# All of v loaded from Pool's queue, and the output tile's pad columns cleared by DVE

## Chip, cores and metric

The kernel runs on 1 core of one Trainium2 chip. The metric is the device time of one execution in microseconds. Before the change the median of 3 runs is 1309.79 us (1308.56 to 1313.95).

## What is computed

Three stages follow each other, all in float32. The change lies in the first.

```python
def _attn_ref(q, k, v):                  # q, k, v: 8 batches, 8 heads, 576 tokens, 64 wide
    chunk = 64
    scores = (q_c @ k_c^T) / sqrt(64)    # within each chunk of 64 tokens
    attn = exp(scores - max) / (sum + 1e-9)
    return attn @ v_c

def _moe_ref(x, w_skip, w_gate, w1, w2): # x: 4608 tokens x 512
    do_compute = x @ w_skip > 0
    e_idx = argmax(x @ w_gate)           # one of 8 experts
    y = gate_w * (relu(x @ w1[e]) @ w2[e])
    return where(do_compute, x + y, x)

def _moe2_ref(x, w_in, w_out):           # 512 -> 2048 -> 512
    h = x @ w_in
    return where(h >= 1, h, where(h <= -1, 0, (h + 1) ** 2 / 4)) @ w_out
```

## The kernel before

**Attention and routing** work on units of 256 tokens, 18 of them (NU), four chunks each. One pass of the loop `for i in range(NU - 1)` handles several units in different steps of their way. s_T transposes q and k of unit i+2 on TensorE and e_T copies them out of PSUM, s_SC makes the scores of unit i+1 and e_SC their exponent on ACT, s_ET and e_ET transpose unit i's exponents, s_AV multiplies them with v of unit i and writes the normalised result into the output tile xn, s_XT transposes xn of unit i-1, s_LG makes the logits of unit i-2. s_SEL and s_RANK choose each token's expert and its place in that expert's list. Their short DVE instructions go into a queue `fill`, from which dve() puts one behind each longer DVE instruction.

**Loads.** load_qk brings q on SP's queue and k on ACT's, two units ahead of their transposes, into tiles with two buffers. load_v brings v on SP's queue: eight loads for a unit, one for each of the four chunks and each parity of the head (line 281), 64 partitions x 4 heads x 64 elements, 64 KB. They go into one of three tiles vbd, in which two heads stand beside each other on a block diagonal, with a column of ones for the sum. load_v(i + 2) stands near the head of pass i; its tile is free once s_AV of unit i-1 has read it.

**The output tile** xn (tag xn, 4 buffers) is 128 partitions x 2 x 516: 512 columns of the token, the gate in column 512 and padding. s_AV gets it and clears columns 512 to 515 with a memset on Pool (line 383); DVE then writes the 512 columns (line 401). Some units later f_gate writes the gate (line 501) and put_x sends the whole tile to x_dram in HBM by a DMA from Pool's queue (line 508). The unit that comes four later needs that buffer again. After the put, f_put scatters the unit's token numbers into the experts' lists, by two indirect DMAs from Pool's queue of 128 single elements each (line 579).

**What sets the order.** The program is written inside `tc.manual_schedule()`: instructions stand on each engine in the order of the code. Each engine works through its own list in order, and a DMA is issued by the engine that it is written on (SP, ACT or POOL), after what that issue waits for. At the start Pool clears a k tile, two of the vbd tiles and some small ones, and issues five small DMAs.

**After attention** come the experts one after another (weights as a sum of two parts, three matmuls for each product), and the last feed-forward stage. They need the routing to be complete.

Of the kernel before, what the change touches and what calls it, by code (L numbers as in the profile page):

```python
# [19 lines left out]
NT, DM = B * S, H * D  # L20
# [7 lines left out]
ROW = DM + 4  # L28
# [58 lines left out]
def kernel(ctx, tc, q, k, v, w_skip, w_gate, w1, w2, w_in, w_out, consts, out):  # L87
    nc = tc.nc
# [16 lines left out]
    def big():  # L105
        return ps.tile([P, 1024], F32, tag="big", name="big", bufs=3)
# [21 lines left out]
    def runs(t0, n):  # L128
        done = 0
        while done < n:  # L130
            b, s = divmod(t0 + done, S)
            step = min(n - done, S - s)
            yield done, step, b, s
            done += step

    def mm(o, l, r, start=True, stop=True):
        nc.tensor.matmul(out=o, lhsT=l, rhs=r, start=start, stop=stop)  # L137
# [120 lines left out]
    T = {}  # L258
# [14 lines left out]
    def load_v(u):  # L273
        if u >= NU:
            return
        for off, n, b, s in runs(u * UNIT, UNIT):
            c0, c1 = off // CH, (off + n) // CH
            for c in range(c0, c1):
                s0 = s + (c - c0) * CH
                for par in range(2):  # L280
                    nc.sync.dma_start(
                        out=vbds[u % NV][64 * par:64 * par + 64, c, :, par, 0:D],
                        in_=v[b, par:H:2, s0:s0 + CH, :].rearrange("h p d -> p h d"),
                    )
# [3 lines left out]
    def dve(n=1):  # L288

        for _ in range(n):  # L290
            if fill:
                fill.pop(0)()
# [83 lines left out]
    def s_AV(u, s):  # L376
        if not 0 <= u < NU:
            return
        et = T["et", u]
        vb = vbds[u % NV]  # L380
        if s == 0:
            T["x", u] = x_p.tile([P, 2, ROW], F32, tag="xn", name="xn", bufs=4)
            nc.gpsimd.memset(T["x", u][:, :, DM:ROW], 0.0)
        xn = T["x", u]
        b = big()
        bg = b.rearrange("p (g w) -> p g w", g=2)[:, :, 0:2 * VW]
        for hp in range(HP):
            for cc in range(2):
                o = (hp % 2) * VW
                mm(  # L390
                    bg[64 * cc:64 * cc + 64, hp // 2, o:o + VW],
                    et[:, s, hp, cc * CH:cc * CH + CH],
                    vb[:, 2 * s + cc, hp].rearrange("p a w -> p (a w)"),
                )
        b4 = bg.rearrange("p g (h w) -> p g h w", w=D + 1)
        rc = r_p.tile([P, 2, H // 2, 1], F32, tag="rc", name="rc")
        nc.vector.tensor_scalar(out=rc, in0=b4[:, :, :, D:D + 1], scalar1=1e-9, scalar2=None, op0=ALU.add)
        dve()
        nc.vector.reciprocal(out=rc, in_=rc)
        dve()  # L400
        nc.vector.tensor_tensor(
            out=xn[:, s, 0:DM].rearrange("p (g h d) -> p g h d", g=2, d=D),
            in0=b4[:, :, :, 0:D],
            in1=rc.to_broadcast([P, 2, H // 2, D]),
            op=ALU.mult,
        )
# [398 lines left out]
    with tc.manual_schedule():  # L805
# [28 lines left out]
        for u, nm, eng in ((0, "qu", nc.scalar), (0, "ku", nc.vector), (1, "qu", nc.scalar)):  # L834
            s_T(u, nm)
            for r in range(2):
                e_T(u, nm, r, eng)
        load_qk(2)
        load_v(0)
        s_T(1, "ku")  # L840
        for r in range(2):
# [4 lines left out]
        nc.gpsimd.tensor_copy(cb, c0[:, C_TRI:C_SEL])  # L846
        load_qk(3)
        load_v(1)
        late = []
        for i in range(NU - 1):  # L850
            s_T(i + 2, "qu")
            s_T(i + 2, "ku")
            load_qk(i + 4, ("qu",))
            load_v(i + 2)
            s_ET(i)
            e_T(i + 2, "qu", 0)
# [15 lines left out]
            if i + 2 == NU:  # L872
                step()
                late.append(fill.pop())
            s_AV(i, 0)
            s_AV(i, 1)
            if i + 2 == NU:
                put_x(i, T["x", i], slice(0, DM))
# [9 lines left out]
        u = NU - 1  # L888
# [10 lines left out]
        run(a[2:6], fill[:3] + r[:1])  # L899
        fill[:] = fill[3:] + a[6:]  # L900
        s_AV(u, 0)
        run(b[:2])
        s_AV(u, 1)
# [380 lines left out]
```

## Time and profile before

| | |
|---|---|
| median of 3 runs | 1309.79 us |
| profiled execution | 1305.73 us, span 1303.9 us |
| TensorE busy | 1238.8 us (95%) |
| DVE, ACT busy | 680.6 us (52%), 662.6 us (51%) |
| POOL busy | 228.9 us (18%), 277 instructions |
| v loads | SP's queue, 144 of 64 KB |
| DMA queues | q1 (SP) 117.30 MB, q10 (ACT) 56.19 MB, q0 (POOL) 28.20 MB |

The span is the time from the first to the last instruction of the profiled execution; the execution's own time is 1.83 us longer. Issuing a DMA is not counted as busy time, except that the rows list each issue with its start and length. In a row of waits the engine named first stood idle until the one behind the arrow was done; where that is a DMA, until the DMA had landed. Queue q1 is SP's, q10 ACT's, q0 Pool's; their rows give packets, MB and the time of these packets as a share of 16 DMA engines.

### The profile page before, as it was taken

To read this page: it belongs to the slowest core of one execution; us is meant where nothing else is said; L and a number is where in the kernel's file an instruction comes from. 1 tells how busy PE (TensorE), PEld (TensorE's weight loads), DVE (VectorE), ACT (ScalarE), POOL (GpSimd) and SP (SyncE) were. 2 spreads that over 40 slices of the span, in tenths; PEclk is the share of its full clock that TensorE was granted. 3 is DMA by queue.
4 is the path that set the end of the run, shared out by engine and by line. 5 is a ranking of instruction groups with operands and counts; after the bars stand their busy time and mean duration, and the time that the engine had idled before them with its cause. 6 is when DMAs were issued, how large, how long until landed. Compare 5 with 4: busy or idle time off the path is not lost.

```text
span 1303.9 us, 19838 instructions
## 1 busy us (share of the span) xinstructions
PE 1238.8 (95%) x7126; PEld 1042.4 (80%) x7128; DVE 680.6 (52%) x1308; ACT 662.6 (51%) x1115; POOL 228.9 (18%) x277
## 2 busy tenths in 40 slices
PE   7987868899999989999999999999999999999998
PEld 6876755789889978888888888887888888888887
DVE  5765686467776691221121120003776687668665
ACT  7875763354444312232223222225787678668764
POOL 3122246434434271011111111000000000000000
PEclk9988996899999999999999999999999999999999
DMA  9989974578776565443344333235343343334431
GB/s 237 232 175 178 189 160 156 124 233 279 218 251 220 170 201 177 161 170 135 132 160 152 119 134 127 108 120 149 111 129 121 114 121 124 119 116 119 127 115 41
DMA packets 163067, 202.98 MB, mean 156 GB/s; under 512 B 51274, under 2 KB 88421, under 8 KB 162966
## 3 DMA queue, kind: packets, MB, share of 16 engines
q1 hardware_dynamic: 107254, 117.30, 33.0%
q10 hardware_dynamic: 45136, 56.19, 12.8%
q0 software_dynamic: 10576, 28.20, 6.4%
q8 instruction: 57, 0.93, 0.3%
q14 instruction: 44, 0.36, 0.1%
HBM read 135.88 MB, written 66.48 MB: 155 GB/s over the span
## 4 chain that ended last, share of the span: by engine, by line
PE 74%; DVE 3%; DMA 2%; issue 1%; ACT 1%; SPq 0%; ACTq 0%; DVEq 0%
PE b L137 30%; PE a L137 30%; PE bank L137 6%; PE big L137 5%; PE t L140 1%; DMA stg<-in_moe_w_dram 1%; DVE a L192 1%; DVE a L191 1%; DMA stg<-in_moe_w_in_dram 1%; DVE s L193 0%; PE t L137 0%; PE big L688 0%; DVE bl L166 0%; DVE hl L717 0%; DMA xs<-x_dram 0%
## 5 line engine op out<-in xcount | busy, mean ns | idle before, releaser
L137 PE MATMUL b<-bh,xh 128*128 128x512 f32 x576 | 225.1, 391 | 1.7 <-ACT xh L1183 1.7
L137 PE MATMUL b<-bh,xl 128*128 128x512 f32 x576 | 225.1, 391 | 0.0
L137 PE MATMUL b<-bl,xh 128*128 128x512 f32 x576 | 224.2, 389 | 0.0
L137 PE MATMUL a<-xh,ah 128*128 128x512 f32 (+1 forms) x576 | 224.0, 389 | 0.0
L1161 ACT COPY hs<-a 128x512 f32<-128x512 f32 x142 | 83.3, 587 | 275.6 <-PE a L137 258.1
L137 PE MATMUL a<-xl,ah 128*128 128x512 f32 (+1 forms) x576 | 222.6, 386 | 0.4 <-DVE xl L1137 0.3
L137 PE MATMUL a<-xh,al 128*128 128x512 f32 (+1 forms) x576 | 222.6, 386 | 0.0
L1184 DVE TENSOR_TENSOR xl<-r,xh 128x512 fp32r<-128x512 f32 x144 | 99.7, 692 | 107.0 <-ACT xh L1183 95.2
L1137 DVE TENSOR_TENSOR xl<-t,xh 128x512 fp32r<-128x512 f32 x34 | 22.0, 687 | 230.3 <-ACT xh L1136 230.3
L137 PEld LDWEIGHTS b<-bh,xh 128*128 128x128 f32 x576 | 108.1, 188 | 26.9 <-ACT xh L1183 5.0
L137 PEld LDWEIGHTS b<-bh,xl 128*128 128x128 f32 x576 | 108.1, 188 | 26.1 <-DVE xl L1184 3.9
L137 PEld LDWEIGHTS b<-bl,xh 128*128 128x128 f32 x576 | 108.1, 188 | 22.2
L137 PEld LDWEIGHTS a<-xl,ah 128*128 128x128 f32 x576 | 108.2, 188 | 22.0 <-DVE xl L1137 0.8
L137 PEld LDWEIGHTS a<-xh,al 128*128 128x128 f32 x576 | 108.2, 188 | 22.0
L137 PEld LDWEIGHTS a<-xh,ah 128*128 128x128 f32 x576 | 108.2, 188 | 21.5 <-ACT xh L1136 0.3
L1173 DVE SCALAR_TENSOR_TENSOR hs<-hs,r 128x512 f32<-128x512 f32 x144 | 99.7, 692 | 46.0 <-DMA hs<-h_dram 46.0
L1183 ACT CAST xh<-r 128x512 fp32r<-128x512 f32 x144 | 89.6, 623 | 51.6 <-PE b L137 32.7
L1177 ACT ACTIVATE hs<-hs,bias 128x512 f32<-128x512 f32 x144 | 104.2, 724 | 0.4 <-ACT hs L1161 0.4
L1172 ACT ACTIVATE r<-hs,bias 128x512 f32<-128x512 f32 x144 | 102.1, 709 | 0.5 <-ACT hs L1161 0.5
L1178 DVE TENSOR_TENSOR r<-r,hs 128x512 f32<-128x512 f32 x144 | 99.8, 693 | 2.6 <-ACT hs L1177 2.0
L204 POOL TENSOR_TENSOR a<-a,bh 128x512 f32<-128x512 f32 x16 | 20.7, 1292 | 267.3 <-ACT bh L203 267.3
L327 ACT COPY qt<-big 64x512 f32<-64x512 f32 x72 | 44.9, 624 | 25.5 <-PE big L140 24.8
(218 smaller groups left out, 2037.3 us busy)
## 6 DMA issues: line engine op xcount, KB each, us to landing
h_dram<-hs ACTq DMA_DIRECT2D x144, 256.0 KB
hs<-h_dram SPq DMA_DIRECT2D x144, 256.0 KB
stg<-in_moe_w_dram SPq DMA_DIRECT2D x128, 256.0 KB
vbd<-in_v_dram SPq DMA_DIRECT2D x144, 64.0 KB
xs<-x_dram SPq DMA_DIRECT2D x17, 512.0 KB
out_dram<-o ACTq DMA_DIRECT2D x34, 256.0 KB
x_dram<-xn POOLq DMA_DIRECT2D x16, 516.0 KB
stg<-in_moe_w_in_dram SPq DMA_DIRECT2D x16, 512.0 KB
```

Of the source, the lines that this page charges most:

```text
L137: nc.tensor.matmul(out=o, lhsT=l, rhs=r, start=start, stop=stop)
L140: nc.tensor.transpose(out=o, in_=i, identity=ident)
L204: nc.gpsimd.tensor_tensor(out=af, in0=af, in1=hi, op=ALU.subtract)
L327: (nc.vector.tensor_copy if eng is nc.vector else nc.scalar.copy)(out=o, in_=b4[64 * r:64 * r + 64, :, par, :])
L1137: nc.vector.tensor_tensor(out=xl[:, :, cut], in0=b3, in1=xh[:, :, cut], op=ALU.subtract)
L1161: nc.scalar.copy(out=hs, in_=b)
L1172: nc.scalar.activation(out=r, in_=h, func=ACTF.Relu, bias=bias[:, 0:1])
L1173: nc.vector.scalar_tensor_tensor(out=h, in0=h, scalar=-1.0, in1=r, op0=ALU.max, op1=ALU.subtract)
L1177: nc.scalar.activation(out=h, in_=h, func=ACTF.Square, scale=0.5, bias=bias[:, 1:2])
L1178: nc.vector.tensor_tensor(out=r, in0=r, in1=h, op=ALU.add)
L1183: nc.scalar.copy(out=gh, in_=r)
L1184: nc.vector.tensor_tensor(out=gl, in0=r, in1=gh, op=ALU.subtract)
```

## The change

load_v issues from Pool's queue, and the memset of the output tile's pad columns runs on DVE.

```diff
             for c in range(c0, c1):
                 s0 = s + (c - c0) * CH
                 for par in range(2):
-                    nc.sync.dma_start(
+                    nc.gpsimd.dma_start(
                         out=vbds[u % NV][64 * par:64 * par + 64, c, :, par, 0:D],
                         in_=v[b, par:H:2, s0:s0 + CH, :].rearrange("h p d -> p h d"),
                     )
...
         if s == 0:
             T["x", u] = x_p.tile([P, 2, ROW], F32, tag="xn", name="xn", bufs=4)
-            nc.gpsimd.memset(T["x", u][:, :, DM:ROW], 0.0)
+            nc.vector.memset(T["x", u][:, :, DM:ROW], 0.0)
```

On Pool, in the middle of the attention loop, the rows before are these (waits in brackets: DMASW and DMAHW are the landing semaphores of DMAs, eight of each kind; DMASW belongs to Pool's DMAs, DMAHW to those of SP and ACT).

```order
L508 DMA x_dram<-xn 128x2x516 [waits DMASW1_49,DVE_49]
L579 DMA idx_dram<-cst,si 36992x1 [waits DVE_49]
L579 DMA idx_dram<-cst,si 36992x1 [waits DMASW3_49]
L383 MEMSET xn 128x2x4 [waits DMASW1_49,PE_49]
L508 DMA x_dram<-xn 128x2x516 [waits DMASW4_49,DVE_49]
```

With the change Pool has the following for one unit, eight v loads (three vbd tiles take turns), a put and two scatters.

```order
L281 DMA vbd_132<-in_v_dram 64x4x64 [waits DMASW4_49,PE_49]
L281 DMA vbd_132<-in_v_dram 64x4x64 [waits DMASW5_49]
L281 DMA vbd_132<-in_v_dram 64x4x64 [waits DMASW6_49,PE_49]
L281 DMA vbd_132<-in_v_dram 64x4x64 [waits DMASW7_49]
L281 DMA vbd_132<-in_v_dram 64x4x64 [waits DMASW0_49,PE_49]
L281 DMA vbd_132<-in_v_dram 64x4x64 [waits DMASW1_49]
L281 DMA vbd_132<-in_v_dram 64x4x64 [waits DMASW2_49,PE_49]
L281 DMA vbd_132<-in_v_dram 64x4x64 [waits DMASW3_49]
L508 DMA x_dram<-xn 128x2x516 [waits DMASW4_49,DVE_49]
L579 DMA idx_dram<-cst,si 36992x1 [waits DMASW5_49,DVE_49]
L579 DMA idx_dram<-cst,si 36992x1 [waits DMASW6_49]
```

The put and the scatters of a unit now stand behind eight v loads, the next eight behind them, and each issue waits for the landing of the one eight ahead of it: the sixth v load for that of the put before it.

On ACT, at the end of the k copies of the same loop, the rows before:

```order
L436 COPY ls<-bank 128x256 [waits PE_49,Activation_49]
L327 COPY kbd_113<-big 64x4x128 [waits Activation_49] x4
L267 DMA ku<-in_k_dram 128x8x128 [waits DMAHW6_49,DMAHW5_49]
L475 ACTIVATE ex<-lm 128x16 [waits DVE_49]
L353 ACTIVATE e<-e 128x512 [waits DVE_49,Activation_49]
```

And with the change:

```order
L436 COPY ls<-bank 128x256 [waits PE_49,Activation_49]
L327 COPY kbd_113<-big 64x4x128 [waits Activation_49] x4
L267 DMA ku<-in_k_dram 128x8x128 [waits DMAHW6_49]
L475 ACTIVATE ex<-lm 128x16 [waits DVE_49]
L353 ACTIVATE e<-e 128x512 [waits DVE_49,Activation_49]
```

The order is the same; the issue of the k load waits for one landing in place of two, and what stands eight ahead of it on SP and ACT together is now a load of q or k.

On DVE, in s_AV of a middle unit, the rows before:

```order
L487 SCALAR_TENSOR_TENSOR oh<-lg,one 128x16 [waits DVE_49]
L397 TENSOR_SCALAR rc<-big 128x8 [waits PE_49]
L493 TENSOR_REDUCE sm<-ex 128x2 [waits Activation_49]
L399 RECIPROCAL rc<-rc 128x8 [waits DVE_49]
L496 TENSOR_SCALAR sm<-sm 128x2 [waits DVE_49]
L401 TENSOR_TENSOR xn<-big,rc 128x512 [waits DMASW6_49,DVE_49]
```

And with the change:

```order
L487 SCALAR_TENSOR_TENSOR oh<-lg,one 128x16 [waits DVE_49]
L383 MEMSET xn 128x2x4 [waits DMASW6_49]
L397 TENSOR_SCALAR rc<-big 128x8 [waits PE_49]
L493 TENSOR_REDUCE sm<-ex 128x2 [waits Activation_49]
L399 RECIPROCAL rc<-rc 128x8 [waits DVE_49]
```

The memset stands ahead of the unit's first division, and the wait for the landing of the put that used this buffer has moved from the write of the tile to the memset.

## Rows read from the trace of the kernel before

**Rows 1.** Windows: engines' busy time, PEclk, DMA share, GB/s, in two stretches.

```profile
core 0: us, PE busy (x) PEld busy (x) DVE busy (x) ACT busy (x) POOL busy (x), PEclk, DMA share, GB/s
32.20:67.45 35.25, 34.42 (x446) 30.30 (x445) 26.37 (x86) 31.81 (x57) 3.83 (x6) 1.00 0.99 227
67.45:171.59 104.14, 85.50 (x1014) 75.46 (x1012) 63.48 (x244) 71.22 (x127) 25.73 (x36) 0.90 0.90 180
```

**Rows 2.** Timeline of TensorE: start, length, instruction, idle before and its end.

```profile
17.97 1.07 PE L140 MATMUL big<-ident,ku 128*128 128x128 f32 x8 [2.76 <-DMA ku<-in_k_dram]
...
32.20 1.04 PE L140 MATMUL big<-ident,qu 128*128 128x128 f32 x8
...
67.45 1.07 PE L140 MATMUL big<-ident,qu 128*128 128x128 f32 x8
...
171.59 1.06 PE L140 MATMUL big<-ident,qu 128*128 128x128 f32 x8 [2.47 <-issue]
```

**Rows 3.** Waits, 0 to 245 us: total us, times, longest.

```profile
PE big L140 <- issue: 17.4, 5, 6.3
...
ACT ex L475 <- DMA vbd<-in_v_dram: 12.2, 4, 6.6
...
DVE xn L401 <- DMA x_dram<-xn: 7.4, 3, 3.4
...
POOL xn L383 <- DMA x_dram<-xn: 46.6, 10, 8.2
```

**Rows 4.** Timelines of ACT and of SP, 107 to 116 us.

```profile
108.19 0.72 ACT L327 COPY kbd<-big 64x512 f32<-64x512 f32 x1
114.89 0.60 ACTq L267 DMA_DIRECT2D ku<-in_k_dram  x1
115.54 0.21 ACT L475 ACTIVATE ex<-lm 128x16 f32<-128x16 f32 x1 [6.63 <-DMA vbd<-in_v_dram]
...
114.55 0.60 SPq L281 DMA_DIRECT2D vbd<-in_v_dram  x1
```

**Rows 5.** Instructions on the tiles vbd: count, ns least/median/most, first and last start.

```profile
L281 SPq DMA_DIRECT2D vbd<-in_v_dram x144: 595/615/3145, 8.2 to 187.1; - x144
...
L814 DVE MEMSET vbd<- x2: 72/72/72, 5.3 to 5.4; 64x16 f32 x2
```

**Rows 6.** Pool's DMA issues: timeline, groups by line, and line 508 by itself.

```profile
49.96 0.78 POOL L508 DMA_DIRECT2D x_dram<-xn  x1 [37.31 <-DVE rc L399]
...
60.41 1.09 POOL L579 DMA_INDIRECT idx_dram<-cst,si  x1 [0.83 <-DMA vbd<-in_v_dram]
61.80 1.03 POOL L579 DMA_INDIRECT idx_dram<-cst,si  x1 [0.30 <-issue]
...
67.79 0.77 POOL L508 DMA_DIRECT2D x_dram<-xn  x1 [3.95 <-DVE sl L563]
...
L579 POOL DMA_INDIRECT idx_dram<-cst,si x36 | 36.9, 1025 | 16.0 <-DVE acc L556 7.8 <-issue 6.9 <-DMA vbd<-in_v_dram 0.8
...
L828 POOL DMA_DIRECT2D w<-in_moe_w_gate_dram x1 | 0.9, 930 | 0.0
...
L832 POOL DMA_DIRECT2D x_dram<-zrow x1 | 0.6, 551 | 0.0
...
L508 POOL DMA_DIRECT2D x_dram<-xn x18: 718/763/790, 50.0 to 218.9; - x18
```

**Rows 7.** Timelines of POOL and DVE where the output tile's buffer comes free.

```profile
55.30 0.10 POOL L383 MEMSET xn<- 128x8 f32 x1 [4.56 <-DMA x_dram<-xn]
...
79.80 0.10 POOL L383 MEMSET xn<- 128x8 f32 x1 [8.16 <-DMA x_dram<-xn]
...
75.10 0.16 DVE L397 TENSOR_SCALAR rc<-big 128x8 f32<-128x8 f32 x1
...
76.24 0.17 DVE L496 TENSOR_SCALAR sm<-sm 128x2 f32<-128x2 f32 x1
79.78 0.69 DVE L401 TENSOR_TENSOR xn<-big,rc 128x512 f32<-128x512 f32 x1 [3.37 <-DMA x_dram<-xn]
```

**Rows 8.** DMA queues, 29 to 31 us: packets, MB, share of 16 engines.

```profile
q1 hardware_dynamic: 1136, 0.27, 81.9%
q10 hardware_dynamic: 38, 0.02, 5.4%
```

**Rows 9.** DMA queues, 51 to 55 us.

```profile
q0 software_dynamic: 144, 0.53, 34.8%
```

**Rows 10.** DMA queues, 62.5 to 70 us.

```profile
q1 hardware_dynamic: 1576, 0.65, 53.7%
q10 hardware_dynamic: 660, 0.34, 51.3%
...
q0 software_dynamic: 63, 0.00, 0.6%
```

## Prediction

> **What bounds the kernel now.** I read the windows view first, to find the stretch that this change can touch: v is loaded during the attention stage only, and the last of the 144 loads is issued at 187.1 us [rows 5]. After that the edit moves nothing, and everything later hangs on the routing that attention produces, so a microsecond won or lost in attention is one at the end. The reader is to see in the two windows that the stage has two halves: up to 67 us TensorE is busy 34.42 of 35.25 us, from there to 171.59 us only 85.50 of 104.14, while the DMA engines stay 0.90 busy and the granted clock falls to 0.90 [rows 1].
>
> Next TensorE's timeline, where each unit of 256 tokens opens with eight transposes of qu. Units open at 32.20, 40.91, 49.76, 58.61 and 67.45: four intervals, 8.81 us each. From 67.45 to 171.59 lie nine intervals (I counted eight openings between these two rows), 11.57 us each [rows 2]. So 9 x (11.57 - 8.81) = 24.8 us is lost, and this is all the change can win in that stretch.
>
> Then the waits, to see who causes the loss. ACT stands 12.2 us in four waits put down to a v load, DVE 7.4 us in three on the landing of the output tile's put, and TensorE's five long idles (17.4 us) follow from these [rows 3]. The timelines show the first kind close up: at 108.91 us ACT is done with kbd, its next instruction is the issue of the second piece of a k load, and that starts at 114.89; SP resumes its v loads at 114.55, in the same moment [rows 4]. The order rows ahead say why: an issue waits for a landing semaphore of its own path, SP and ACT take theirs from one set (DMAHW), and eight v loads a unit use that set up. So ACT's exponent stands behind a k load, which stands behind landings of v. The second kind is a buffer: the put issued at 67.79 frees its tile at 79.80, which is when DVE writes the next one [rows 6, 7].
>
> Why landings are late: in 62.5 to 70 us the Pool queue moved 63 small packets and the two hardware queues, 51.3% and 53.7% busy, moved under 1 MB in 7.5 us [rows 10], after two scatters issued at 60.41 and 61.80 [rows 6]. The scatters stay as they are.
>
> **The change part by part.** *SP loses 144 v issues* of 615 ns [rows 5], 4.9 us a unit. SP is not waited for except through q, so by itself this is worth 0; the cover is the loads' lead of two units. The q loads go out earlier, and in the start the bytes are the same with the DMA engines at full share, so the 2.76 us that TensorE waits there for ku [rows 2] I leave standing (gain between 0 and 2.8).
>
> *ACT's k loads* no longer share semaphores with v. The 12.2 us go, unless something is late next; what is late next is Pool.
>
> *Pool gains 8 loads a unit.* The trace has no v load on Pool, so its price is bounded by the rows of Pool's other issues: 0.551 us for a tiny one, 0.763 for the put (256 rows), 0.930 for the gate weights (512 rows), 1.025 for an indirect one [rows 6]. A v load moves 64 x 4 = 256 rows, like the put, so I take 0.763. A unit then costs Pool 8 x 0.763 = 6.10, the put 0.76, two scatters 2.05, and 0.30 of issue before each of these three, 0.90: **9.8 us**. That is above TensorE's 8.81, so Pool sets the pace of the second half. On top come landing waits. Eleven issues share eight semaphores, so the sixth v load waits for the put's landing and the eighth for the second scatter's. The put has taken from 49.96 to 55.30, 5.3 us, at best and from 67.79 to 79.80, 12.0, at worst [rows 6, 7]. Pool reaches the sixth load some 7.2 us after the put, so at best nothing is added, and at 12.0 the unit takes 12.0 + 3 x 0.763 = 14.3. In the middle, 8.65 + 2.3 = 10.9. I take 10.4 us, nearer to the low end, because v no longer crowds the put from the other queue.
>
> What Pool's order allows: the v loads of unit i+2 stand behind the put and the scatters of unit i-1's round, and are needed two units later, over 15 us away, so their delay is covered. The put behind the v loads is not covered as well: its tile is rewritten one unit later, 8.81 us, of which landing takes 5.3, so 3.5 us of lateness are free.
>
> *Packets.* In 29 to 31 us, when almost only v moves, 1136 packets of SP's queue took 81.9% of 16 engines for 2 us: 23 ns for 256 bytes [rows 8]. In 51 to 55 us a put of 256 rows of 2064 bytes went as some 128 packets (16 of the 144 only signal): two rows in one, 0.348 x 64 / 144 = 155 ns each [rows 9]. If Pool's path also packs v, 512 KB a unit cost at most 512/4.1 = 125 packets, 125 x 155 / 16 = 1.2 us in place of 2048 x 23 / 16 = 2.9; if not, the same 2.9. Either way it lies under Pool's 9.8, so it counts 0 in the sum; it is why I trust the landings not to get worse.
>
> *The pad memsets* move to DVE: 18 of some 0.07 us (a DVE memset of vbd took 72 ns), 1.3 us of DVE that is busy 63.48 of 104.14 us: between 0 and 1.3, taken as 0 [rows 1, 5]. Its wait for the put's landing sits four short DVE instructions ahead of the write that waits for it now, and these start within 1.2 us at most [rows 7], so the wait moves and does not grow. Off Pool it matters more: there 46.6 us of waiting for the put's landing [rows 3] would have stood ahead of every round of v loads.
>
> A rule that speaks against the edit is in the Trainium skill, SBUF — State Buffer, section "SBUF: two separate sides": while DVE runs an instruction from SBUF to SBUF in a two-port mode, GpSimd cannot write descriptors, and transfers issued by it stand still. The trace of this stage does not show it: 18 puts were issued in 718 to 790 ns each [rows 6] beside a DVE that was busy for 61% of the second half [rows 1]. By the rule each load could stretch by a DVE instruction; by the row the stretch is nil, and I take nil.
>
> **Sum.** Nine units at 10.4 in place of 11.57: -10.5. Pool carries its full eleven issues from about the unit that opens at 49.76, so two units ahead of 67.45 build up 2 x (10.4 - 8.81) = 3.2 us of lateness, of which 3.5 are free; I charge half, +1.5. Total -9.0. The profiled execution took 1305.73 us, so 1296.7; the median of the runs shown, 1309.79, is 4.06 above it, which gives **1301** (rounded).
>
> **Rivals.** *(a) Pool is the new bound and dearer than the put says.* At 1.03 us a load, the indirect row, a unit costs 8 x 1.03 + 0.76 + 2.05 + 0.90 = 12.0, with 0.6 for landings 12.6: 9 x 1.0 = +9.4, and 2 x 3.8 - 3.5 = +4 before. That is +13.5, or 1323. It decides from 0.89 us a load: 8 x 0.89 + 3.71 + 0.6 = 11.4, where the nine units win 9 x 0.17 = 1.5 and the two early ones lose 2 x 2.6 - 3.5 = 1.7. For it speaks the 0.930 us row; against it the 0.763 us of the same number of rows. *(b) No difference that can be told*, about 1308: the put's landing paces the unit at 10.9 to 11.5 because the scatters set it, or the 12.2 us come back as waits for the put. The Trainium skill, DMA: Bandwidth & Descriptors, section "Issuing engines are not separate DMA queues", says that all issuers run on the same 16 DMA engines and that another issuer saves only the sequencer's time; [rows 10] agree as to the engines, since both hardware queues slow down behind Pool's scatters. *(c) All of the loss goes*: 9.8 us a unit without landing waits and with the early ku: 9 x 1.77 + 2.8 = -18.7, 1291. That the loads do not move at all is excluded by the order rows.
>
> **How the numbers follow.** Forecast 0.45, (c) 0.10, (b) 0.22, (a) 0.23. A measurement here tells about 0.5% from no change, 6.5 us, so faster (under 1303.2) holds the forecast and (c) less a few cases that fall short, 0.53; same is (b) with these, 0.23; slower is (a) and a little of (b), 0.24. The range goes from (c) with its noise, 1289, to just short of all of (a), 1322.
>
> **What would show it.** Right: ACT's 12.2 us put down to v gone; v issues on Pool of about 0.76 us; the nine intervals near 10.4 us; Pool without the long idles; the DVE memset holding the put's wait. Wrong: v issues of 0.9 us or more, Pool busy without a gap and units of 12 us or more; or long waits of DVE's memset on the put, each of several us.

## Result: slower, 1325.53 us in place of 1310.85

The changed kernel took 1325.53 us (median of 4 runs, 1323.17 to 1327.74); the kernel before, on the same chip, 1310.85 (4 runs). The ratio is 1.0116, 95% interval 1.0082 to 1.0151. The forecast of 1301 was wrong in sign, and the range, which ended at 1322, did not hold the time.

The profiled execution took 1323.17 us with a span of 1321.4, against 1303.9 before: 17.5 us more. The windows view of the changed kernel, cut at its own openings of units, answers to [rows 1]:

```profile
core 0: us, PE busy (x) PEld busy (x) DVE busy (x) ACT busy (x) POOL busy (x), PEclk, DMA share, GB/s
35.41:70.73 35.32, 34.61 (x444) 30.32 (x445) 26.68 (x91) 31.34 (x56) 23.42 (x37) 1.00 0.94 206
70.73:184.23 113.50, 86.20 (x1014) 76.95 (x1013) 63.45 (x252) 71.52 (x127) 70.25 (x99) 0.88 0.76 161
184.23:213.87 29.64, 18.71 (x210) 16.34 (x210) 21.15 (x75) 14.88 (x28) 19.95 (x23) 0.79 0.71 159
```

The first half of the stage runs as before, 8.83 us a unit. The nine units behind it take 113.50 us, 12.6 each, against 104.14 and 11.57. TensorE's work in them is the same (86.20 us against 85.50) and the DMA engines are less busy on average, 0.76 against 0.90: over the stretch as a whole neither is short, somebody waits. The last row is the end of the stage, up to the moment in which TensorE transposes the first expert's list. It took 25.39 us before (from 171.59 [rows 2] to 196.98). Where the time went, in TensorE's timeline of the changed kernel:

```profile
24.86 1.07 PE L137 MATMUL big<-vbd,et 128*64 128x130 f32 x14 [2.73 <-DMA vbd<-in_v_dram]
25.86 1.70 PE L140 MATMUL big<-ident,qu 128*128 128x128 f32 x8
...
70.73 1.07 PE L140 MATMUL big<-ident,qu 128*128 128x128 f32 x8
87.96 1.94 PE L140 MATMUL big<-ident,qu 128*128 128x128 f32 x8 [8.23 <-issue]
...
184.23 1.94 PE L140 MATMUL big<-ident,qu 128*128 128x128 f32 x8 [2.88 <-issue]
213.87 0.58 PE L137 MATMUL bank<-ident,il 3*128 3x3 f32 x2 [9.69 <-DVE t L553]
```

The unit that opened at 67.45 us opens at 70.73, +3.3. Nine units later it is 184.23 in place of 171.59, so the nine cost +9.4. The end grew from 25.4 to 29.6, +4.2. That is 16.9 of the 17.5 us. The list's row at 213.87 names DVE's t (line 553), and DVE was late for it by one wait that the kernel before does not have in its end:

```profile
207.21 0.15 DVE L397 TENSOR_SCALAR rc<-big 128x8 f32<-128x8 f32 x1 [4.22 <-issue]
```

The 4.22 us are its memset's wait for the landing of the put issued at 200.86. (SP's reading of the list, line 609, may start only when the loop's scatters have landed; it moved too, from 191.97 to 207.76, but the row does not name it.)

The waits of the changed kernel, 0 to 245 us, answer to [rows 3]:

```profile
DVE rc L397 <- issue: 31.9, 6, 8.1
...
PE big L140 <- issue: 26.7, 5, 8.2
POOL vbd L281 <- PE bank L137: 14.8, 6, 6.0
...
POOL vbd L281 <- DMA vbd<-in_v_dram: 10.9, 12, 2.2
...
POOL vbd L281 <- DMA idx_dram<-cst,si: 9.1, 4, 3.6
...
POOL vbd L281 <- DMA x_dram<-xn: 6.6, 3, 3.3
```

ACT's 12.2 us behind v landings are gone. In their place DVE stands 31.9 us ahead of line 397 (its memset of the pad columns is issued just ahead of that line and waits for the put's landing), and TensorE 26.7 us behind DVE. Pool's v loads wait too, 41 us in these four rows. How one feeds the other stands in Pool's timeline from 62 us on:

```profile
62.15 0.72 POOL L508 DMA_DIRECT2D x_dram<-xn  x1 [3.03 <-DVE sl L563]
63.71 1.09 POOL L579 DMA_INDIRECT idx_dram<-cst,si  x1 [0.84 <-DVE acc L556]
65.10 1.02 POOL L579 DMA_INDIRECT idx_dram<-cst,si  x1 [0.30 <-issue]
66.12 3.81 POOL L281 DMA_DIRECT2D vbd<-in_v_dram  x6
75.94 1.25 POOL L281 DMA_DIRECT2D vbd<-in_v_dram  x2 [6.01 <-PE bank L137]
77.15 0.74 POOL L508 DMA_DIRECT2D x_dram<-xn  x1
...
80.58 1.95 POOL L281 DMA_DIRECT2D vbd<-in_v_dram  x3
83.03 1.23 POOL L281 DMA_DIRECT2D vbd<-in_v_dram  x2 [0.51 <-DMA vbd<-in_v_dram]
86.98 1.83 POOL L281 DMA_DIRECT2D vbd<-in_v_dram  x3 [2.71 <-DMA x_dram<-xn]
88.80 0.72 POOL L508 DMA_DIRECT2D x_dram<-xn  x1
```

Six v loads go out at once; the seventh and eighth, which take the landing semaphores of the two scatters issued at 63.71 and 65.10, go out only at 75.94, 11.1 us after the first of these scatters was issued in full (64.80). The row names TensorE, whose semaphore the seventh load also waits for, because its tile must have been read. But the last product with v had ended at 69.40 (67.45 + 1.95), and the next one ended after the load went out:

```profile
67.45 1.95 PE L137 MATMUL big<-vbd,et 128*64 128x130 f32 x32
...
76.30 1.96 PE L137 MATMUL big<-vbd,et 128*64 128x130 f32 x32
```

So the tile was free, and what the load still waited for was the landing. The put behind them goes out at 77.15; before, the put in that place had gone out at 67.79 [rows 6]. It then takes some 9.6 us to land, and DVE's memset and Pool's next v loads are released together:

```profile
86.74 0.15 DVE L397 TENSOR_SCALAR rc<-big 128x8 f32<-128x8 f32 x1 [8.12 <-issue]
86.75 0.07 DVE L383 MEMSET xn<- 128x8 f32 x1
```

The price of the issues was not the trouble; the tile view of vbd answers to [rows 5]:

```profile
L281 POOL DMA_DIRECT2D vbd<-in_v_dram x144: 615/636/704, 11.8 to 196.5; - x144
```

A v load costs Pool 0.636 us, less than the 0.763 taken for it.

### The profile page after: what moved, and what is told of

Same layout as the page of the kernel before. It is cut to its first block, busy times and chain, and to the rows that moved or that the text cites. A ratio compares the mean times of both kernels' runs of the same rounds, so it can differ in the third digit from the quotient of the medians.

```text
span 1321.4 us, 19863 instructions
## 1 busy us (share of the span) xinstructions
PE 1242.0 (94%) x7127; PEld 1045.3 (79%) x7128; DVE 678.9 (51%) x1326; ACT 663.3 (50%) x1115; POOL 317.8 (24%) x403
## 4 chain that ended last, share of the span: by engine, by line
PE 81%; DMA 6%; issue 4%; DVE 3%; POOL 3%; ACT 2%; ACTq 0%; SPq 0%; POOLq 0%; DVEq 0%
PE b L137 30%; PE a L137 29%; PE bank L137 8%; PE big L137 7%; PE big L140 4%; DMA stg<-in_moe_w_dram 2%; ACT qt L327 1%; DMA vbd<-in_v_dram 1%; PE t L140 1%; DMA idx_dram<-cst,si 1%; DVE a L192 1%; DVE a L191 1%; POOL al L166 1%; DMA stg<-in_moe_w_in_dram 1%; POOL idx_dram L579 1%
## 5 line engine op out<-in xcount | busy, mean ns | idle before, releaser
L137 PEld LDWEIGHTS b<-bl,xh 128*128 128x128 f32 x576 | 108.5, 188 | 22.4
L281 POOL DMA_DIRECT2D vbd<-in_v_dram x144 | 89.6, 647 | 45.0 <-PE bank L137 14.8
```

Of the source, the lines that this page charges most:

```text
L281: nc.gpsimd.dma_start(out=vbds[u % NV][64 * par:64 * par + 64, c, :, par, 0:D], in_=v[b, par:H:2, s0:s0 + CH, :].rearrange("h p d -> p h d"),)
```

## The experiments

Two theories stood after this. The **coupling theory**: v, put and scatters share Pool's queue and its eight landing semaphores, so late landings of scatters hold v loads, these hold the put, and the put's late landing holds DVE. The **transfer theory**: the 16 DMA engines deliver so much and no more, whoever issues. Later runs add rivals of their own. Units are numbered from 0. In the table "unit 8 opens" is TensorE's opening of that unit by qu (67.45 us in the kernel before), "units" the mean of the nine intervals from there to the opening of unit 17 (171.59), and "end" the time from that one to the transposes of the first list, all from the profiled execution of each.

| run | unit 8 opens, us | units, us | end, us | ratio to before |
|---|---|---|---|---|
| before | 67.45 | 11.57 | 25.4 | |
| the change | 70.73 | 12.61 | 29.6 | 1.0116 [1.0082, 1.0151] |
| pad_on_dve_alone | 68.16 | 11.66 | 25.7 | 1.0009 [0.9986, 1.0031] |
| v_on_pool_alone | 70.81 | 12.64 | 30.0 | 1.0090 [1.0065, 1.0116] |
| put_on_sp | 69.44 | 10.89 | 31.8 | 0.9987 [0.9957, 1.0016] |
| half_v_on_pool | 72.27 | 11.07 | 25.8 | 0.9955 [0.9930, 0.9980] |
| first_v_on_sp | 75.57 | 12.16 | 26.4 | 1.0135 [1.0086, 1.0184] |
| last_v_on_sp | 68.78 | 12.20 | 25.6 | 1.0078 [1.0045, 1.0111] |
| no_early_scatters | 70.35 | 8.85 | 22.3 | (1286.64, one run) |
| four_v_tiles | 69.77 | 12.18 | 27.0 | (1315.21, one run) |
| before_no_early_scatters | 67.40 | 8.85 | 22.4 | (1280.06, one run) |
| middle_v_on_pool | 72.42 | 11.97 | 24.8 | 1.0080 [1.0049, 1.0111] |
| half_v_from_unit_3 | 68.92 | 9.77 | 26.5 | 0.9951 [0.9932, 0.9970] |
| half_v_and_put_on_sp | 68.33 | 10.24 | 25.3 | 0.9909 [0.9889, 0.9930] |
| five_output_tiles | 71.32 | 10.54 | 33.2 | (1321.91, one run) |
| two_staging_tiles | 68.65 | 12.47 | 26.2 | (1326.11, one run) |

A profile is one execution; the ratios are of medians, to runs of the kernel before on the same chip (1310.25 us beside runs 1 to 4, 1304.83 beside 5 to 8, 1306.46 beside 9 to 12, 1302.35 beside 13 and 14). Times of different groups are therefore compared by their ratios. How far one trace can be trusted: last_v_on_sp, five_output_tiles and two_staging_tiles leave the first units of the change as they are, and unit 8 opens at 68.78, 71.32 and 68.65 us in them; the first and the last of these, with units of 12.20 and 12.47 beside the change's 12.61, leave most of the middle as it is too. A difference between two single traces that is no larger than these tells nothing.

**1. The memset alone.**

```diff
-            nc.gpsimd.memset(T["x", u][:, :, DM:ROW], 0.0)
+            nc.vector.memset(T["x", u][:, :, DM:ROW], 0.0)
```

> The pad memset on DVE, v left on SP. Coupling theory (the loss comes from v, the put and the scatters sharing Pool's queue and its eight landing semaphores): the memset costs nothing, 1310 us, within 0.4% of before, nine units from about 67 us at 11.6 us each. Rival, memset theory (DVE stands at the head of the unit for the put's landing, where before only the tile's write stood): most of the loss is here, 1318 us or more.

Measured: 1311.53 us, units of 11.66. By itself this half of the change costs and brings nothing that can be told.

**2. v on Pool alone**, the memset left on Pool.

```diff
-                    nc.sync.dma_start(
+                    nc.gpsimd.dma_start(
```

> v on Pool, the pad memset left on Pool. Coupling theory: slower than the full change, since the memset's wait for the put's landing (46.6 us of it before) now stands in Pool's queue ahead of the next put and the v loads: 1330 to 1345 us. Memset theory: as before the change or faster, 1305 to 1312 us.

Measured: 1323.07 us, units of 12.64, as in the whole change. Neither theory's number: the memset on Pool, which I had thought would stand ahead of the v loads and make it worse still, adds nothing that can be told. The loss comes from the loads. The wait only shows under another name: DVE stands 25.7 us at line 401 for the put's landing.

**3. The put on SP**, all else as in the change.

```diff
-        (nc.gpsimd if cut.start == 0 else nc.scalar).dma_start(out=rows, in_=xn[:, :, cut])
+        (nc.sync if cut.start == 0 else nc.scalar).dma_start(out=rows, in_=xn[:, :, cut])
```

> The full change with the put of the output tile issued by SP in place of Pool. Coupling theory: the put no longer stands behind v loads that wait for the scatters' landings, so DVE's wait at the memset (31.9 us in six) goes, the units fall from 12.6 to 10 to 11 us, the whole to 1300 to 1312 us. Rival, transfer theory (landings are late because Pool's ring is served one packet after the other and the scatters stall all engines, whoever issues the put): units stay at 12 us or more, 1320 to 1327 us.

Measured: 1309.17 us, units of 10.89: the same bytes, one issue a unit on another queue, and 1.7 us a unit less. The put that went out at 77.15 and released DVE's memset 9.6 us later in the change goes out at 69.36 here and releases it at 77.61, 8.2 us later: most of what it gains is its issue, and its landing is still late. The transfer theory does not hold alone. The end grew to 31.8 us, though, so 1309.17 is no more than level with the kernel before. In that end DVE waits 3.42 us for a put and then spends 7.85 us in one short instruction (line 574, 0.16 us at the median), while Pool works through six TENSOR_TENSOR (190.77 to 198.14); in the kernel before the longest such instruction of DVE beside Pool's took 5.57 us.

**4. Half of v on Pool**, the odd heads' loads; the even heads' go back to SP.

```diff
-                    nc.gpsimd.dma_start(
+                    (nc.gpsimd if par else nc.sync).dma_start(
```

> One parity of v on Pool, the other on SP: seven Pool issues a unit, fewer than the eight semaphores. Coupling theory: the put waits for no landing of its own unit's round any more; units of 10.3 to 11.2 us, 1298 to 1308 us, faster than before and than the change. Transfer theory: halfway between the two kernels, 1316 to 1320 us.

Measured: 1305.87 us, units of 11.07. With four v loads, a put and two scatters Pool issues seven DMAs a unit on eight semaphores, and it is 0.45% below the kernel before, with an interval that does not reach 1, although its units open 4.8 us later at the start.

**5. v of the first unit on SP.**

```diff
-                    nc.gpsimd.dma_start(
+                    (nc.sync if u == 0 else nc.gpsimd).dma_start(
```

> The change, with the eight v loads of unit 0 alone given back to SP. Queue theory of the start (v of unit 0 lands late because Pool issues it behind its own clearing and five small DMAs, which makes TensorE wait 2.73 us at the first product with v and the units open 3.3 us late): the third unit opens near 23.5 us in place of 25.9, the unit that opens at 70.7 opens at 67.2 to 68.5, and the time is 3 us less than the change's, 1320 to 1322. Rival (the start is late because v shares the DMA engines in any case, or because v of units 1 and 2 is packed and lands in one piece): the unit still opens at 70 or later and the time stays at 1323 to 1326. The nine units behind it stay at 12.4 to 12.8 us in both.

Measured: 1323.35 us; the units open later still, at 75.57. The rival was right. TensorE no longer waits for v of unit 0 but for a k load, as its timeline shows:

```profile
19.51 1.06 PE L140 MATMUL big<-ident,ku 128*128 128x128 f32 x8 [3.38 <-DMA ku<-in_k_dram]
31.86 1.94 PE L140 MATMUL big<-ident,ku 128*128 128x128 f32 x8 [5.71 <-DMA ku<-in_k_dram]
```

From 14 to 24 us the DMA engines are full. In the kernel before SP's q and v and ACT's k share them, with Pool's queue idle:

```profile
q1 hardware_dynamic: 4161, 1.28, 68.4%
q10 hardware_dynamic: 2339, 1.17, 47.5%
...
q0 software_dynamic: 64, 0.00, 0.4%
```

In run 5 Pool's queue takes part of that time for v of the units to come, and the k loads move 0.77 MB in place of 1.17, although the last two before TensorE's long wait were issued no later (21.55 and 22.29 us against 21.70 and 23.75):

```profile
q1 hardware_dynamic: 2388, 0.85, 50.5%
q10 hardware_dynamic: 1545, 0.77, 45.3%
q0 software_dynamic: 317, 0.58, 26.6%
```

SP's next q loads go out earlier there as well, since no v stands between them, so the share that Pool's loads have in the delay is not separated.

**6. v of the last two units on SP.**

```diff
-                    nc.gpsimd.dma_start(
+                    (nc.sync if u >= NU - 2 else nc.gpsimd).dma_start(
```

> The change, with the v loads of the last two units (16 and 17) given back to SP. Queue theory of the end (the last put and scatters of the loop stand on Pool behind v loads that wait for landings, so the list of the first expert is read 16 us later and TensorE waits 9.7 us for it): from the last opening by qu to the first transposes of the list 25 to 27 us in place of 29.6, the time 3 to 5 us less than the change's, 1319 to 1322. Rival (the end is longer because DVE's own work stands behind the late units, or because the list's landing is late by the scatters themselves): 29 us or more, 1323 to 1326. Start and middle units as in the change, 70.7 us and 12.4 to 12.8 us a unit.

Measured: 1316.21 us, a ratio of 1.0078 where the change has 1.0116, and the end 25.6 us in place of 29.6. DVE's wait of 4.22 us in the end is gone. The queue theory of the end stands, by a landing: in the change DVE had written the gate for the put of 200.86 at 195.30, Pool was through with its v loads at 197.16, and what the put still waited for, besides that gate, was the semaphore of the v load eight ahead of it, issued at 190.61.

**7. The change without the first twelve units' scatters.**

```diff
-            for s in range(n):
+            for s in range(n if u >= NU - LATE else 0):
```

> The change without the scatters of the first twelve units' token numbers (24 of 36 indirect DMAs), so the lists of the experts are incomplete. Only the attention stage is read. Landing theory (issues on Pool wait for the late landings of scatters and of the put behind them): without scatters the put lands in some 5 us, no issue on Pool waits, Pool needs 8 x 0.64 + 0.76 = 5.9 us a unit, and the units behind 70 us fall to 8.8 to 9.4 us until the scatters begin again with the thirteenth unit, DVE's memset waits under 5 us in all. Tile theory (the v loads wait for TensorE to free their tile, and hold the put): the units stay at 11 us or more and the rows of vbd waiting on PE stay near 15 us.

Measured, in the windows view from 70.35 us on, nine units:

```profile
70.35:150.01 79.66, 77.77 (x1014) 68.52 (x1013) 63.44 (x254) 70.61 (x126) 50.83 (x81) 1.00 0.93 228
```

8.85 us a unit, TensorE busy 77.77 of 79.66 us at full clock, with all of v and the put on Pool. The landing theory stands: nine issues a unit on Pool are no bound, and without scatters no row of DVE waiting for a put is left. (The run takes the scatters' own two issues away too, 2.1 us a unit.)

**8. Four v tiles.**

```diff
-    NV = 3
+    NV = 4
```

> The change with four v tiles in place of three (two more memsets at the start). Tile theory (14.8 us of Pool's v loads are put down to TensorE's products with v, whose tile they overwrite, and the put stands behind them): that wait goes, units fall from 12.6 to 10.5 to 11.5 us, and the time to 1308 to 1315. Landing theory (the engine named there had long been done, and the issue waited for the landing of the one eight ahead on Pool): the units stay at 12.2 to 13.0 us, the same waits appear under the names of DMAs, and the time is 1320 to 1328.

Measured: units of 12.18 us, a hair under the landing theory's 12.2 to 13.0 and far from the 10.5 to 11.5 of the tile theory. The time, 1315.21 us in one run, is under the landing theory's range and at the upper edge of the tile theory's; beside its own kernel before (1304.83) it is 0.8% longer, where the change is 1.2%. The waits from 0 to 265 us decide it:

```profile
DVE rc L397 <- issue: 21.1, 4, 8.0
...
POOL vbd L281 <- DMA idx_dram<-cst,si: 20.4, 8, 5.3
...
POOL vbd L281 <- PE bank L137: 2.0, 2, 1.1
```

The row that named TensorE (14.8 us in the change) has shrunk to 2.0, and the waits for the scatters grew from 9.1 to 20.4 us. TensorE had been named because its semaphore stands on the same instruction; what came last was, in most of that time, a scatter's landing: 10.9 of the 14.8 us stand at the seventh load of a round (75.94, 121.76 and 172.38 us), the one that takes a scatter's semaphore.

**9. The kernel before without the early scatters**, the edit of run 7 made in it.

> The kernel before (v on SP, memset on Pool) without the scatters of the first twelve units' token numbers; lists incomplete, only the attention stage is read. Scatter theory (the scatters are what makes v land late on SP's path and the put on Pool's, in both kernels): the nine units from the opening near 67 us take 8.8 to 9.1 us each as in the change without scatters (8.85), ACT's waits put down to v fall under 2 us. Rival (in the kernel before, the eight v loads and k loads crowd their own landing semaphores, scatters or not): units of 10 us or more, ACT's waits on v 8 us or more.

Measured: 8.85 us a unit here too, and no row of ACT waiting for v. So the 24.8 us that the kernel before loses in these units come from the scatters as well; v on SP is late only because of them.

**10. v on Pool in the middle alone**, units 3 to 15.

```diff
-                    nc.gpsimd.dma_start(
+                    (nc.gpsimd if 2 < u < NU - 2 else nc.sync).dma_start(
```

> The change with v of units 0, 1, 2 and of 16, 17 given back to SP, so Pool loads v of units 3 to 15. Crowding theory of the start (Pool issues v of units 1 and 2 from 12 us on, earlier than they are needed, and their packets delay the k loads): the third unit opens at 23.5 to 24.5 us, that of the change's 70.73 at 67 to 68.5. The middle stays at 12.0 to 12.8 us a unit, the end at 25 to 26 us; sum 1306 + 0.8 x 9 to 1306 + 1.2 x 9, 1311 to 1318 where before is 1309. Rival (the start is late because Pool's path lands late in any case, or the middle's loss comes from lateness that the start hands on): start as in the change, 69 us or later, or a middle under 11.6 us.

Measured: 1316.07 us, 9.6 above the kernel before beside it, where the crowding theory gave 2 to 9. Unit 3 opens at 23.33 us as in the kernel before. But unit 5 opens at 44.66 us (40.91 there), after TensorE has waited 1.19 us for a v load and 2.28 for a q load; Pool had issued its first 22 loads between 22.8 and 42.6 us. The delay was not removed, it moved to where Pool's loads begin. The opening of unit 8, 72.42, missed the 67 to 68.5 expected. The middle (11.97) and the end (24.8) came out a little under what was expected.

**11. Half of v on Pool from unit 3 on.**

```diff
-                    nc.gpsimd.dma_start(
+                    (nc.gpsimd if par and u > 2 else nc.sync).dma_start(
```

> As the run with the odd heads' v loads alone on Pool, but from unit 3 on; units 0 to 2 all from SP. Crowding theory: the start goes back by 3 to 5 us (unit opens at 67 to 69 in place of 72.3), the middle stays near 11.1 us, the end near 25.8, so 0.6 to 0.8% below the kernel before (the run with half was 0.45% below). Rival (the early part is lost again in the middle, since the scatters set a time by which each unit is done): the middle grows to 11.5 us and the time is 0.3 to 0.5% below before.

Measured: 1300.12 us (median of 12 runs), ratio 0.9951, the interval 0.9932 to 0.9970. The start comes back as expected (68.92), but the ratio is that of run 4: by the medians what the start gave was lost again, as the rival said. The profiled execution, with units of 9.77, was one of the faster ones (1295.15; the 12 runs lie between 1292.52 and 1306.50), so its middle need not be typical, and this pair stays undecided.

**12. The same with the put on SP** (the edits of runs 11 and 3 together).

> As half_v_from_unit_3, with the put issued from SP. Pool then has four v loads and two scatters a unit, six issues on eight semaphores. Queue theory: no put stands behind a scatter's landing on Pool, the middle falls to 10.3 to 10.9 us, but the end grows (31.8 us with the put on SP in the run before), so the time is 0.5 to 1.2% below before. Transfer theory (the scatters hold the 16 DMA engines, so who issues the put matters not): middle 11.0 to 11.5, 0.2 to 0.7% below before.

Measured: 1294.44 us, ratio 0.9909 [0.9889, 0.9930], better than the kernel before and the change. Pool issues four v loads and two scatters a unit; DVE waits 8.5 us in all for puts:

```profile
DVE rc L397 <- issue: 8.5, 2, 5.5
...
PE big L140 <- issue: 8.3, 2, 5.4
```

The ratio is in the queue theory's range, and 5.7 us below run 11 by the medians. But the traces do not show that the put's place won them: the middle is 10.24 us here and was 9.77 in run 11, and TensorE transposes the first list at 185.87 us, later than in run 11 (183.32), so what makes this span 4.7 us shorter lies behind the attention stage. Both profiles are among the faster executions of their kernels. The end did not grow this time (25.3 us); DVE has no wait for a put in it, and no instruction over 1.3 us.

**13. Five output tiles**, with two staging tiles of the experts' weights to make room.

```diff
-NSTG = 3
+NSTG = 2
...
-            T["x", u] = x_p.tile([P, 2, ROW], F32, tag="xn", name="xn", bufs=4)
+            T["x", u] = x_p.tile([P, 2, ROW], F32, tag="xn", name="xn", bufs=5)
```

> The change with five buffers of the output tile in place of four, and to make room with two staging tiles of the experts' weights in place of three; the attention stage is read. Buffer theory (the late puts cost time because the unit four later needs their tile: DVE's memset waits 27.7 us in five, TensorE stands 26.7 us in five behind it): with one unit more of slack DVE's memset waits under 8 us in all and the nine units fall from 12.6 to 9.5 to 11 us. Rival (Pool's own round of eleven issues and their landings is longer than a unit, so the put falls further behind with each unit and a fifth tile only delays it): units of 11.8 us or more, memset waits of 18 us or more.

Measured: the units fall to 10.54, as the buffer theory says, but the first three of the nine run at 8.85 to 9.01 and the other six at 11.33, and DVE's waits sum to 16.8 us, between the two. Against run 14 the nine units win 17.4 us, and 7.0 of it are lost in the end, 33.2 us against 26.2, where TensorE waits for the list itself:

```profile
199.36 0.56 PE L137 MATMUL bank<-ident,il 3*128 3x3 f32 x2 [12.41 <-DMA il<-idx_dram]
```

Pool's puts went out at 62.72 and at 191.17 us with ten between them, 11.7 us apart: Pool's round is longer than a unit with or without the fifth tile. So both links are there: the tile is the way by which the loss reaches TensorE, Pool's round is what sets its size, and a fifth tile delays it.

**14. Two staging tiles alone**, as the measure for run 13.

> The change with two staging tiles of the experts' weights and the four output tiles kept, as the measure beside the run with five. If staging plays no part in the attention stage, the nine units stay at 12.2 to 13.0 us and the memset waits at 20 to 30 us; if the weights' staging crowds the queues there, units of 11.8 us or less.

Measured: units of 12.47, memset waits of 28.8 us: the staging plays no part in the attention stage. (The time, 1326.11 us against 1302.35 of the kernel before beside it, is further off than that of the change. From the first list to the last instruction it takes 1117.2 us where the change takes 1107.5, so the experts seem to miss the third tile; run 13 carries that too, and its total is not compared.)

## Why the prediction was wrong

*Right: what is lost and by whom.* Both waits that it named in the kernel before are real, and 24.8 us was the loss: run 9 gives it back in full, with units of 8.85 us. ACT's 12.2 us went, as forecast.

*Right, and on the good side: the price of an issue.* 0.636 us against 0.763 taken, so rival (a), Pool dearer by the load, gave nearly the right time (1323) by luck: its mechanism did not happen. The Trainium skill's rule in SBUF — State Buffer, section "SBUF: two separate sides", counted as nil, is not seen in the issues either: 704 ns is the longest of 144.

*Right: the memset.* Run 1 measures no difference, and the put's wait moved to it.

*Right: packets.* The prediction asked whether Pool's path packs v. It does:

```profile
DMA packets 128508, 202.99 MB, mean 154 GB/s; under 512 B 14410, under 2 KB 51557, under 8 KB 128406
...
q1 hardware_dynamic: 68086, 107.85, 29.0%
...
q0 software_dynamic: 15184, 37.65, 10.8%
```

In the kernel before there were 163067 packets, 107254 on q1 and 10576 on q0. So 9.45 MB of v, 36864 rows of 256 bytes, left q1 with 39168 packets fewer and came to q0 with 4608 more. But from fewer packets I took that landings would be no worse, and that does not follow: what lands late are the scatters, which are the same, and what lands with them.

*The step that failed: the landing waits.* The prediction gave Pool 9.8 us a unit of issues, and for landings on top it chose: "I take 10.4 us, nearer to the low end". With the measured prices the issues of a round come to 8 x 0.636 + 0.74 + 1.05 + 1.02 = 7.9 us and some 0.3 to 0.9 of gaps between them. Pool's puts went out at 77.15 and 200.86 with nine between them: a round took 12.4. So Pool waited about 3.6 to 4.2 us a round, nearly all for landings by the rows above, where 0.6 had been taken. The prediction's own upper end, 14.3 a unit, came from a put that lands in 12.0 us, and its middle, 10.9, from 8.65; the mistake was to choose below the middle. The reason given, that "v no longer crowds the put from the other queue", is what run 9 speaks against: the lateness comes from the scatters, which the prediction itself had named as the cause and then left out of this term. It priced the wait of the sixth load for the put, and named that of the eighth load for the second scatter without a price. It was those waits, 9.1 us under the scatters' name and 10.9 of the 14.8 under TensorE's, that held the put back (run 8).

*The put "not covered as well".* The prediction gave the put 3.5 us of free lateness and charged 1.5 us for the two units ahead of the nine. That charge was not due: from 35.41 to 70.73 the units run at 8.83 us. But the put at 77.15 was 9.4 us later than the one in its place before, 6.1 more than the start's 3.3, and DVE stood 8.1 us for it and TensorE 8.2. The wait that the prediction listed as its sign of being wrong, long waits of DVE's memset on the put, is what came: 31.9 us in six.

*The start, taken as 0 (gain 0 to 2.8): +3.3.* The working said that bytes are the same and the engines full, so nothing changes. In runs 5 and 10 k and q land later while Pool's loads move beside them, so it seems to matter whose bytes go first. With v on Pool from unit 0, 1 or 3 on, all of it or half, unit 8 opens at 68.33 to 75.57 us in thirteen traces; with v on SP, at 67.40 to 68.16 in three. Which packets went ahead of which was not tried, so the cause of this term stays open.

*The end, "nothing": +4.2.* Not looked at. It is DVE's wait of 4.22 us for a put, and run 6 puts it down to v loads ahead of that put on Pool.

*Rival (b)*, no difference, leaned on the Trainium skill, DMA: Bandwidth & Descriptors, section "Issuing engines are not separate DMA queues": one saves the sequencer's time only. Run 3 goes against that reading: moving one issue a unit from Pool to SP took 1.7 us off each unit, with the same bytes on the same engines (272 packets a put in place of 144). What it saved was mainly its place behind late landings, since it went out 7.8 us earlier and took 8.2 us in place of 9.6 to land.

The sum, forecast and measured: start 0 and +3.3, the units ahead of the nine +1.5 and 0, the nine -10.5 and +9.4, the end 0 and +4.2; together -9.0 and +16.9. Of the 25.9 us between them the nine units make 19.9.

## What to carry to other kernels

Before moving loads to another queue, write out that queue's round in order and give every issue the landing it waits for, the slowest transfer on the queue first: here eleven issues a round on eight landing semaphores took 12.4 us where the issues alone cost 7.9. A slow transfer (here scatters of single elements) did less harm on a queue whose round has fewer issues than there are semaphores (run 4), and what others wait for (the put) did better off that queue (run 3): half of v on Pool and the put on SP made the loads' move worth 0.9%. And in a stretch where the DMA engines are full, an earlier issue of one load can go with a later landing of another (runs 5 and 10).

## Not expected of the hardware

- Two scatters of 128 single elements a unit cost 3.8 us a unit in the changed kernel and 2.7 in the one before: leaving out 24 of 36 brought the nine units from 12.6 to 8.85 us in the changed kernel and from 11.57 to 8.85 in the one before, with v, put, q and k unchanged.
- The load that waits for the landing of one went out 11.1 us after that scatter's issue, and the put issued at 77.15 us, ahead of the next two scatters, took 9.6 to land. Why a scatter takes so long to land, no run here tells.
- After TensorE's idle of 8.23 us the eight transposes of qu took 1.94 us, at a granted clock of 0.50 (87.96 to 89.69 us), where they take 1.07 at 1.00: the lower of its two clock levels, 1.2 in place of 2.4 GHz. So this long stall cost somewhat more than its length. The granted clock of the end was 0.79, against 0.95 before.
- The same load of 256 rows of 256 bytes went as about one packet a row from SP's queue (39168 packets fewer for 36864 rows) and as 32 a load from Pool's (4608 for 144 loads).
